# First batch's attention scores by quarters of the array, and another order of the steps ahead of the first up product

## The chip, the core and the metric

The kernel runs on one core of one Trainium2 chip. The core has TensorE (PE, with its weight loads shown as PEld), VectorE (DVE), ScalarE (ACT), GpSimd (POOL) and SyncE (SP), which here issues all loads and stores. Each engine takes its instructions in the order in which the program lists them. The metric is the device time of one execution in microseconds, lower is better.

## What is computed

Four batches of 768 tokens. Each goes through an attention of 8 heads with 64 channels, in which a token sees the tokens nearer than 16 and 24 block summaries (the maximum of 32 keys and the mean of 32 values), and then through two multiplications over tokens (rank 32) and channels (512 to 2048 and back):

```python
k_sum = k.reshape(B, H, nb, block, D).max(axis=3)
v_sum = v.reshape(B, H, nb, block, D).mean(axis=3)
scores_l = scale * np.matmul(q, k.transpose(0, 1, 3, 2))      # kept where |i - j| < 16
scores_s = scale * np.einsum('bhsd,bhnd->bhsn', q, k_sum) + np.log(block)
a = softmax(concat(scores_l, scores_s)); x = a @ concat(v, v_sum)
h = xt @ U @ V
u = x + h.transpose(0, 2, 1)
out = u + np.maximum(u @ w_ch1, 0.0) @ w_ch2
```

`U`, `V`, `w_ch1` and `w_ch2` come as 64-bit floats, and the kernel turns them into 32-bit ones itself.

## The kernel before

The work falls into stages by batch. Batch 0's attention stands ahead of everything; behind it come 16 rounds, one for each 128 hidden channels, that multiply batch 0 by the up and down weights (lines 920 and 942) while the weights are turned from 64 bits, split and stored, and while batch 1's attention goes on between the products. Batches 1 to 3 then run from the stored weights (lines 1203 and 1288).

What matters here is the part ahead of the first up product, the prologue. Its order is a list of words, `START` (line 69), that the program works through one after the other; each word makes the instructions of one step, and on each engine they stand in that order. A word is a step and its numbers:

- `lk`, `lq`, `lv`: SP loads one head's keys, one head's queries (two transfers) or two heads' values (two transfers). `lm`, `li`, `lr`, `lu`: mask, identity, a replication matrix, and U with V. `la`, `lb`: one block of 128 hidden channels of the up or of the down weights, 512 KB each, ten of them in the list.
- `K`: DVE takes the block maxima of a head's keys (line 319). `Kp` and `Kd`: POOL or DVE copies them into the gaps of the key tile (line 336).
- `S`: PE makes scores (line 354) into a bank of PSUM; a word stands for half a head, three tiles of 128 queries by 120 keys. `E`: DVE masks half a head's scores and takes the minimum (line 403), ACT takes the exponentials (line 413). `T`: PE transposes them (line 463). `C`: ACT copies them out (line 469). `V`: PE multiplies them by the values (line 480). `N`: DVE normalises a head (lines 506 to 508).
- `M` and `Mo`: PE makes the block means of two heads' values (line 293), ACT copies them out (line 307). `B` and `D` with `p`, `d` or `a`: POOL, DVE or ACT spreads them into the value tiles (line 340).
- `X`, `Xt`, `Xs`, `Xl`: U and V are scaled by ACT (line 149), turned by POOL (line 162) and DVE (lines 168, 171), and split. `Q`, `Qo`, `I`, `Io`, `J`, `Jo`, `G`, `Go`: the multiplication over tokens; `Q`, `I`, `J`, `G` are on PE (lines 1015, 666, 684, 700 and 708), the `o` steps copy out on ACT (lines 1026, 679, 692, 720) and take the rest on DVE (lines 694, 721).
- `Z`: ACT scales the weights of one round (line 149). `Y`: DVE turns them in three steps (lines 164, 168, 171). `W`: ACT rounds and DVE subtracts (lines 186, 187).
- `U0.0`: the first up product (line 920), twelve matmuls.

The queries of a head lie in a tile of 128 partitions of which every other block of 64 by 64 is zero, so that a matmul over 128 partitions gives two half tiles of 64 queries with their own keys. The function `scores` uses this: six matmuls of 128x128 weights and 120 columns for a head. A second function, `scores_by_subtiles`, leaves the zeros out: it makes 12 matmuls of 64x64 weights and 120 columns for a head, each placed on one quarter of the array, and writes two banks. Before the change only batches 2 and 3 use it (line 377 of the profile), and batch 1 uses `scores` as batch 0 does. An fp32 matmul shows as two in the profile, so a head is 12 instructions at line 354 and 24 at line 377.

The query tiles of batch 0 are four, used by heads h and h+4, so that head 7's load waits until head 3's scores are done. PSUM has 8 banks, handed out by whichever is free.

Of the kernel before, what the change touches and what calls it, by code (L numbers as in the profile page):

```python
# [16 lines left out]
B, H, S, D = 4, 8, 768, 64  # L17
DM, DF, R = 512, 2048, 32
P = 128
# [4 lines left out]
KC = NB + W  # L24
# [26 lines left out]
I32 = mybir.dt.int32  # L51
# [15 lines left out]


START = """
    lk2 lk0 K2 K0 lk1 Kp2 lq0 Kd0 li S0 lm S1 K1 lq1 Kp1 S2 lq2 S3 F lk3 E0 T0 E1 E2 S4 C0 lq3 K3 T1  # L70
    E3 E4 T2 S5 Kp3 S6 C1 S7 E5 lk4 T3 E7 lv0 K4 M0 lk5 Mo0 T4 T7 lq4 Kp4 lu C3 S8 S9 C4 lq5 T5 E6
    C2 Bp1 Dd0 X K5 Bp0 V1 T6 Dd1 E9 lv2 Kp5 Xt0 S11 E8 S10 V0 lv1 V2 E11 V3 M2 T9 E10 lk7 Mo2 lk6
    Xt1 N0 T11 lq7 C5 T8 Bp4 Xt2 lq6 M1 Dp4 lv3 C9 T10 C8 C11 C7 K7 Kp7 V9 C10 S15 Dd5 Bp5 K6 C6 Kp6
    S14 Mo1 Dp2 S12 Bp3 S13 Xs Dp3 V10 la0 la1 lb0 N1 E15 E14 V7 V6 V11 V8 T15 Bp2 la4 M3 E13 T14
    E12 Z0 T13 N5 lb1 Mo3 T12 N3 Y0.0 Xl lb2 C15 Ba7 C14 V4 Dp7 V15 V5 lr N4 Y0.1 Q0 N2 C12 Z1 Qo0
    V14 lb4 I2 N7 Io2 C13 Q1 Y0.2 Bp6 I1 Y1.0 Qo1 J2 Dp6 Jo2 la3 V12 V13 Io1 N6 Y1.1 I0 G1.2 la2 Io0
    J1 J0 I3 Jo1 Jo0 G0.2 Io3 J3 G0.1 W0 Jo3 Go0.2 Go0.1 G1.1 G0.0 G1.0 Go1.1 G0.3 Go0.0 Go0.3 Y1.2
    Go1.2 Go1.0 G1.3 Go1.3 Z2 U0.0 lb3 W1
"""


# [5 lines left out]
def body(ctx: ExitStack, tc, q0, q1, k, v, vn, uv, w1, w2, mask, ident, rep, out):  # L87
# [114 lines left out]
    def load_k(st, h):  # L202

        if st.b == 0:
            kt = kt0[h]
        else:
            kt = kv.tile([P, KTW], F32, name="kt")
        nc.sync.dma_start(out=pairs_of(kt), in_=k[st.b, :, h])
        st.kt[h] = kt

    def load_q(st, h):

        st.qt[h] = qz0[h % 4] if st.b == 0 else qz[h % 2]
        nc.sync.dma_start(out=st.qt[h][:64, 1::2], in_=q0[st.b, :, h])
        nc.sync.dma_start(out=st.qt[h][64:, 0::2], in_=q1[st.b, :, h])

    def load_qk(st, h):
        load_k(st, h)
# [5 lines left out]
    def pairs_of(kt):  # L224
        return kt[:, NB:].rearrange("p (i c) -> p i c", c=KP)[:, :, : 2 * W]
# [137 lines left out]
    def scores_by_subtiles(st, h):  # L363

        st.neg[h] = small.tile([P, NU], F32, name="neg")
        qt, kt = st.qt[h].rearrange("p u q -> p (u q)"), st.kt[h]
        ps = [bank("ps_s") for _ in range(2)]  # L370
        for i in range(3):
            for s in range(2):
                for a in range(2):
                    j = ORDER.index(2 * i + a)
                    q0, k0 = 64 + j * P + 64 * s, (j // 2) * KP + (j % 2) * KC
                    r, c = 64 * ((s + a) % 2), 64 * s
                    nc.tensor.matmul(  # L377
                        ps[a][c : c + 64, i * KC : (i + 1) * KC],
                        qt[r : r + 64, q0 : q0 + 64],
                        kt[r : r + 64, k0 : k0 + KC],  # L380
                        start=True,
                        stop=True,
                        tile_position=(r, c),
                    )
# [36 lines left out]
    def tiles_of(e):  # L421
        return e[:, : NU * KC].rearrange("p (u k) -> p u k", k=KC)
# [34 lines left out]
        nc.scalar.copy(at, ps[:KC, : 3 * P].rearrange("k (u i q) -> k u i q", i=4, q=32))  # L457

    def transposes(st, h, a):
        e = tiles_of(st.e[h])[:, 3 * a : 3 * a + 3]  # L460
        ps = bank("ps_t")
        for i in range(3):
            nc.tensor.transpose(ps[:KC, i * P : (i + 1) * P], e[:, i, :], ident_sb)  # L463
        st.ps_t[h, a] = ps

    def copies(st, h, a, copy):
# [4 lines left out]
    def values(st, h, a):  # L471
        at = st.at.pop((h, a))
        if h not in st.psx:
            st.psx[h] = bank("ps_x")
        ps = st.psx[h]
        vt = st.vt[h]
        for i in range(3):
            u = 3 * a + i
            for t in range(2):
                nc.tensor.matmul(  # L480
                    ps[64 * t : 64 * t + 64, u * DV : (u + 1) * DV],
                    at[:, i, 64 * t : 64 * t + 64],
                    vt[u % 2][:, (u // 2) * 2 + (t + u) % 2],
                    start=True,
                    stop=True,
                )
# [541 lines left out]
    def step(f):  # L1028
        return lambda i: f(st, i // 2, i % 2)

    acts = {
        "lk": lambda h: load_k(st, h),
        "lq": lambda h: load_q(st, h),
        "lm": lambda: nc.sync.dma_start(out=mask_sb, in_=mask),
        "li": lambda: nc.sync.dma_start(out=ident_sb, in_=ident),
        "lr": lambda: nc.sync.dma_start(out=rep_sb, in_=rep),
        "lv": lambda p: load_v_pair(st, p),
        "lu": lambda: nc.sync.dma_start(out=raw_uv, in_=uv.bitcast(I32)),
        "la": lambda f: load_weight(0, f),
        "lb": lambda f: load_weight(1, f),  # L1040
        "Q": spread_v,
# [399 lines left out]
```

## Time and profile before

| | |
|---|---|
| median of 3 runs | 666.86 us (666.3 to 669.9) |
| the profiled execution | 668.33 us, of which 666.5 us are its span |
| first score matmul on PE | 8.01 us |
| first up product on PE | 52.80 us |
| PE busy 10 to 35 us, 35 to 50 us | 22.15 of 25 us, 14.35 of 15 us |

Times in the profile count from the start of the span. A row of the timeline gives start, length, engine, line, operation, tiles and count, and in brackets how long the engine was idle ahead of it and what ended that. A row of the stages gives the length, then the busy time of PE, PEld, DVE, ACT and POOL with their instructions, the granted TensorE clock, the share of the 16 DMA engines in use and the GB/s that they moved. A matmul's shown length runs into the next one's, so a block's cost is taken from its start to the start of what follows.

### The profile page before, as it was taken

How to read it: one execution, taken by the hardware profiler on the slowest of the kernel's cores; microseconds unless marked ns; L12 is line 12 of the kernel's file. 1: busy time of each engine (PE TensorE's matmuls, PEld its weight loads, DVE VectorE, ACT ScalarE, POOL GpSimd, SP SyncE). 2: the span in 40 equal slices, each digit the busy share in tenths (PEclk: the TensorE clock that was granted, in tenths of full speed). 3: DMA queues.
4: the chain of work that ended last, by engine and by line, in shares of the span. 5: the costliest groups of instructions: out<-in, count | busy, mean ns of one | idle time of the engine just before them, and what ended most of it. 6: DMA issues, size and time to landing. Idle time of an engine off the chain costs nothing.

```text
span 666.5 us, 14015 instructions
## 1 busy us (share of the span) xinstructions
PE 640.6 (96%) x5232; PEld 562.6 (84%) x5232; DVE 371.7 (56%) x1006; ACT 358.5 (54%) x803; POOL 361.0 (54%) x402
## 2 busy tenths in 40 slices
PE   5899999999999898999999999999999999999997
PEld 4789889988888797997787899997787899998885
DVE  5578866668777763567544645566644521232223
ACT  4666666655553555765453467665453365553322
POOL 5424975965577676762336487662334375653310
PEclk9999999999999998999999999999999999999999
DMA  8997497766774268787457059787441055331002
GB/s 219 228 367 239 135 315 240 230 173 195 227 225 163 72 178 265 213 251 203 147 142 205 25 171 325 228 247 204 138 143 59 24 171 178 112 126 64 32 1 94
DMA packets 76420, 116.13 MB, mean 174 GB/s; under 512 B 6976, under 2 KB 52928, under 8 KB 76352
## 3 DMA queue, kind: packets, MB, share of 16 engines
q1 hardware_dynamic: 76352, 115.24, 57.1%
q8 instruction: 41, 0.67, 0.4%
q14 instruction: 27, 0.22, 0.1%
HBM read 91.10 MB, written 24.12 MB: 173 GB/s over the span
## 4 chain that ended last, share of the span: by engine, by line
PE 83%; DVE 4%; DMA 4%; ACT 3%; POOL 2%; issue 2%; SPq 1%; ACTq 0%; POOLq 0%; DVEq 0%
PE acc L1288 30%; PE ps_h L1203 25%; PE acc L942 7%; PE ps_h L920 7%; PE ps_x L494 3%; PE ps_s L354 2%; PE ps_o L739 2%; PE ps_s L377 2%; DMA place<-in_uv 1%; DMA place<-in_q 1%; PE ps_m L666 1%; DMA whole<-up 1%; PE ps_t L463 1%; PE ps_x L480 1%; POOL place L187 1%
## 5 line engine op out<-in xcount | busy, mean ns | idle before, releaser
L187 POOL TENSOR_TENSOR parts<-whole,parts 128x512 fp32r<-128x512 f32 (+1 forms) x144 | 180.5, 1262 | 160.4 <-ACT parts L186 151.3
L1288 PE MATMUL acc<-parts,gh 128*128 128x512 f32 x576 | 192.3, 399 | 0.0
L1203 PE MATMUL ps_h<-op,parts 128*128 128x384 f32 x1008 | 187.5, 340 | 3.2 <-ACT place L1262 2.9
L1203 PEld LDWEIGHTS ps_h<-op,parts 128*128 128x128 f32 x1008 | 175.4, 189 | 6.2 <-ACT place L1262 3.2
L1288 PEld LDWEIGHTS acc<-parts,gh 128*128 128x128 f32 x576 | 108.1, 188 | 23.7 <-issue 1.7
L1288 PE MATMUL acc<-parts,gl 128*128 128x512 f32 x288 | 112.6, 391 | 0.0
L1273 DVE SCALAR_TENSOR_TENSOR gl<-place,gh 128x768 fp32r<-128x768 f32 x48 | 56.2, 1171 | 97.1 <-ACT gh L1272 97.1
L186 ACT CAST parts<-whole 128x512 fp32r<-128x512 f32 (+1 forms) x144 | 83.6, 584 | 9.9 <-DMA whole<-up 8.2
L920 PE MATMUL ps_h<-place 128*128 128x384 f32 x384 | 74.5, 342 | 0.0
L1272 ACT ACTIVATE gh<-place 128x768 fp32r<-128x768 f32 x48 | 40.6, 846 | 60.0 <-PE acc L1288 59.9
L413 ACT ACTIVATE e<-e,neg 128x120 f32<-128x120 f32 x144 | 46.3, 386 | 47.4 <-DVE neg L403 45.7
L942 PE MATMUL acc<-place,gh 128*128 128x512 f32 x192 | 68.4, 410 | 1.3 <-POOL place L187 1.3
L920 PEld LDWEIGHTS ps_h<-place 128*128 128x128 f32 x384 | 65.9, 188 | 1.0 <-DVE place L721 0.3
L162 POOL TENSOR_SCALAR val<-place 128x512 f32<-128x512 f32 (+1 forms) x30 | 47.0, 1582 | 30.8 <-ACT place L149 14.2
L1288 PEld LDWEIGHTS acc<-parts,gl 128*128 128x128 f32 x288 | 54.2, 188 | 9.9 <-DVE gl L1273 0.3
L187 POOL TENSOR_TENSOR place<-val,place 128x512 fp32r<-128x512 f32 x29 | 39.4, 1378 | 18.6 <-ACT place L186 15.3
L187 POOL TENSOR_TENSOR op<-tmp,op 128x384 fp32r<-128x384 f32 x24 | 25.4, 1067 | 39.2 <-ACT op L186 39.2
L942 PEld LDWEIGHTS acc<-place,gh 128*128 128x128 f32 x192 | 35.6, 188 | 10.5 <-POOL place L187 3.2
L403 DVE CUSTOM_DVE_ANT_0 e<-ps_s,mask_sb 128x120 f32<-128x120 f32 x144 | 32.5, 276 | 13.3 <-PE ps_s L377 8.5
L942 PE MATMUL acc<-place,gl 128*128 128x512 f32 x96 | 37.6, 392 | 0.0
L932 ACT ACTIVATE gh<-ps_h 128x384 fp32r<-128x384 f32 x32 | 15.7, 490 | 36.4 <-PE ps_h L920 36.0
L1263 DVE TENSOR_TENSOR place<-place,ps_h 128x384 f32<-128x384 f32 x24 | 13.3, 553 | 38.4 <-ACT place L1262 38.3
(124 smaller groups left out, 858.8 us busy)
## 6 DMA issues: line engine op xcount, KB each, us to landing
place<-in_w SPq DMA_DIRECT2D x32, 512.0 KB, 5.6
whole<-up SPq DMA_DIRECT2D x24, 512.0 KB, 3.9
whole<-down SPq DMA_DIRECT2D x24, 512.0 KB, 3.7
whole<-up SPq DMA_DIRECT2D x24, 384.0 KB, 3.3
vt<-in_v SPq DMA_DIRECT2D x48, 146.2 KB, 4.1
kt<-in_k SPq DMA_DIRECT2D x24, 288.0 KB, 5.4
out_t<-o SPq DMA_DIRECT2D x32, 192.0 KB, 2.2
there<-squares SPq DMA_DIRECT2D x16, 384.0 KB, 4.4
```

The costliest lines, as they stand in the source:

```text
L162: nc.gpsimd.tensor_scalar(f32(bits), f32(hi), 0.0, None, ALU.mult)
L186: nc.scalar.copy(hi, val)
L187: engine.tensor_tensor(lo, val, f32(hi), ALU.subtract)
L403: nc.vector.tensor_tensor_reduce(out=e[:, u, :], in0=ps[:, i * KC : (i + 1) * KC], in1=mask_sb[:, m, :], scale=-SCALE, scalar=BIG, op0=ALU ...
L413: nc.scalar.activation(e[:, u, :], e[:, u, :], AF.Exp, bias=st.neg[h][:, u : u + 1], scale=-1.0,)
L494: nc.tensor.matmul(ps[32 * i : 32 * i + 32, u * DV : (u + 1) * DV], at[:KC, i, u], vt[u % 2][:, (u // 2) * 2 + (i // 2 + u) % 2], start=Tr ...
L920: nc.tensor.matmul(ps[:, :NH], w_split[0, f][:, c % 2, part_w, c // 2], ut[:, c, :], start=(n == 0), stop=(n == 3 * NC - 1),)
L942: nc.tensor.matmul(acc[t], gt[:, sl], w_split[1, f][:, part_w], start=(first and j == 0), stop=(last and j == 2),)
L1203: nc.tensor.matmul(ps, a[:, sa, i], b[:, sb, i], start=(first and n == 0), stop=(n == 5), skip_group_check=not first,)
L1272: nc.scalar.activation(gh, h, AF.Relu)
L1273: nc.vector.scalar_tensor_tensor(gl, h, 0.0, f32(gh), ALU.max, ALU.subtract)
L1288: nc.tensor.matmul(acc[t], gt[:, sl], w[:, part_w], start=(f == 0 and j == 0), stop=(f == NF - 1 and j == 2),)
```

## The change

The word `S` now makes a whole head with `scores_by_subtiles`, so that eight `S` words remain, all even. The transposes and the value products take their tiles in the order in which that function lays them out (`tiles_in_bank`). The list `START` is another one: other order of heads (1, 0, 3, 2, 5, 4, 7, 6), U and V loaded seventh instead of after the queries of head 4, no copy of key maxima or value summaries on DVE, and the weights loaded in another order. The loaders get an argument for the issuing engine, which stays SP. The diff without the moved numbers of lines (of `START` only its first and last lines are shown):

```diff
-    lk2 lk0 K2 K0 lk1 Kp2 lq0 Kd0 li S0 lm S1 K1 lq1 Kp1 S2 lq2 S3 F lk3 E0 T0 E1 E2 S4 C0 lq3 K3 T1
...
-    Go1.2 Go1.0 G1.3 Go1.3 Z2 U0.0 lb3 W1
+    lk1 lk0 K1 K0 lq1 Kp1 lq0 S2 lm lu li X E3 lk3 Kp0 lk2 S0 Xt0 E2 F lq3 K3 E0 Kp3 lk5 K2 Kp2 T3
...
+    Jo3 G0.2 Go0.0 G0.1 Go0.2 G0.3 Go0.1 G1.3 Go0.3 G1.1 W0 G1.2 Y1.2 Go1.1 Go1.0 lb4 Go1.2 Go1.3
+    U0.0 W1 Z2
...
     def tiles_in_bank(st, a):
-        return [3 * a + i if st.b < 2 else 2 * i + a for i in range(3)]
+        return [3 * a + i if st.b == 1 else 2 * i + a for i in range(3)]
...
     def transposes(st, h, a):
-        e = tiles_of(st.e[h])[:, 3 * a : 3 * a + 3]
+        e = tiles_of(st.e[h])
         ps = bank("ps_t")
-        for i in range(3):
-            nc.tensor.transpose(ps[:KC, i * P : (i + 1) * P], e[:, i, :], ident_sb)
+        for i, u in enumerate(tiles_in_bank(st, a)):
+            nc.tensor.transpose(ps[:KC, i * P : (i + 1) * P], e[:, u, :], ident_sb)
...
     def values(st, h, a):
-        for i in range(3):
-            u = 3 * a + i
+        for i, u in enumerate(tiles_in_bank(st, a)):
...
-        "S": step(scores),
+        "S": lambda i: scores_by_subtiles(st, i // 2),
```

On PE, from the last heads' scores (line 354 before, 377 after) to the last value products (480 before, 479 after) it stood like this; line 463 is a transpose, 293 the block means, 1015 and 1014 `Q`, 666 and 665 `I`, 684 and 683 `J`:

```order
L354 MATMUL ps_s<-place 128x120 x12
L480 MATMUL ps_x<-place 64x65 x30
L463 MATMUL ps_t<-ident_sb,gl 120x128 x3
L293 MATMUL ps_n<-place,means_w 32x65 x24
L463 MATMUL ps_t<-ident_sb,gl 120x128 x3
L463 MATMUL ps_t<-ident_sb,gh 120x128 x6
L480 MATMUL ps_x<-place 64x65 x18
L1015 MATMUL ps_v<-place,ident_sb 32x192 x8
```

and now:

```order
L377 MATMUL ps_s<-place 64x120 x12
L463 MATMUL ps_t<-ident_sb,gh 120x128 x3
L463 MATMUL ps_t<-ident_sb,gl 120x128 x3
L293 MATMUL ps_n<-place,means_w 32x65 x24
L463 MATMUL ps_t<-ident_sb,gl 120x128 x3
L463 MATMUL ps_t<-ident_sb,gh 120x128 x3
L479 MATMUL ps_x<-place 64x65 x36
L665 MATMUL ps_m<-x,u_sb 32x128 x12
L463 MATMUL ps_t<-ident_sb,gh 120x128 x3
L683 MATMUL ps_r<-t_785,rep_sb 128x128
L479 MATMUL ps_x<-place 64x65 x12
L1014 MATMUL ps_v<-place,ident_sb 32x192 x16
```

Between the last scores and the last block means stood 30 value products, and now none; behind the last block means stand 48 (36 and 12) where there were 36 (18, and 18 further on).

On DVE, around the last head's normalising (lines 506 to 508 before, 505 to 507 after) the queue stood like this; 164, 168 and 171 turn weights, 694 and 721 belong to the multiplication over tokens, 187 splits the first up weights:

```order
L171 SCALAR_TENSOR_TENSOR val<-place,val 128x512
L164 TENSOR_SCALAR val<-place 128x512 x2
L694 TENSOR_TENSOR t_st<-ps_r,t_st 64x128
L506 TENSOR_SCALAR sum<-ps_x 128x6
L507 RECIPROCAL sum<-sum 128x6
L508 TENSOR_TENSOR x<-ps_x,sum 128x6x64
L168 SCALAR_TENSOR_TENSOR val<-place,val 128x512 x2
L694 TENSOR_TENSOR t_st<-ps_r,t_st 64x128 x2
L187 TENSOR_TENSOR place<-val,place 128x2x256
L694 TENSOR_TENSOR t_st<-ps_r,t_st 64x128
L721 TENSOR_TENSOR place<-ps_u,place 128x384 x5
```

and now:

```order
L505 TENSOR_SCALAR sum<-ps_x 128x6
L506 RECIPROCAL sum<-sum 128x6
L507 TENSOR_TENSOR x<-ps_x,sum 128x6x64
L164 TENSOR_SCALAR val<-place 128x512 x2
L693 TENSOR_TENSOR t_st<-ps_r,t_st 64x128
L168 SCALAR_TENSOR_TENSOR val<-place,val 128x512 x2
L693 TENSOR_TENSOR t_st<-ps_r,t_st 64x128 x2
L171 SCALAR_TENSOR_TENSOR val<-place,val 128x512
L693 TENSOR_TENSOR t_st<-ps_r,t_st 64x128
L720 TENSOR_TENSOR place<-ps_u,place 128x384 x4
L187 TENSOR_TENSOR place<-val,place 128x2x256
```

The two sign steps, one `L171` and one `t_st` step stand behind the last normalising now instead of ahead of it.

On ACT, around the first up product's gate (`gh<-ps_h`), the scaling of the round 2 weights (line 149) stood ahead of it:

```order
L720 CAST place<-ps_u 128x384 x8
L149 ACTIVATE place<-place 128x512 x2
L932 ACTIVATE gh<-ps_h 128x384
L186 CAST place<-val 128x512
L186 CAST place<-val 128x2x256
L932 ACTIVATE gh<-ps_h 128x384
```

and now it stands behind the gate and the two roundings of the round 1 weights:

```order
L186 CAST place<-val 128x2x256
L719 CAST place<-ps_u 128x384 x4
L931 ACTIVATE gh<-ps_h 128x384
L186 CAST place<-val 128x512
L186 CAST place<-val 128x2x256
L149 ACTIVATE place<-place 128x512 x2
L931 ACTIVATE gh<-ps_h 128x384
```

On POOL the first turning step of round 2 (line 162) waits for that scaling, and the round 2 split follows from it.

More of the change, by code (lines that the diff above doesn't have):

```diff
@@ L200, in new_batch, with load_k @@
         return st
-    def load_k(st, h):
+    def load_k(st, h, by=nc.sync):
         if st.b == 0:
@@ L207, in load_k, with load_q @@
             kt = kv.tile([P, KTW], F32, name="kt")
-        nc.sync.dma_start(out=pairs_of(kt), in_=k[st.b, :, h])
+        by.dma_start(out=pairs_of(kt), in_=k[st.b, :, h])
         st.kt[h] = kt
-    def load_q(st, h):
+    def load_q(st, h, by=nc.sync):
         st.qt[h] = qz0[h % 4] if st.b == 0 else qz[h % 2]
-        nc.sync.dma_start(out=st.qt[h][:64, 1::2], in_=q0[st.b, :, h])
-        nc.sync.dma_start(out=st.qt[h][64:, 0::2], in_=q1[st.b, :, h])
+        by.dma_start(out=st.qt[h][:64, 1::2], in_=q0[st.b, :, h])
+        by.dma_start(out=st.qt[h][64:, 0::2], in_=q1[st.b, :, h])
     def load_qk(st, h):
@@ L1031, in body @@
     acts = {
[L1032 to L1035, printed above, removed]
+        **{
+            key: load
+            for e, by in (("l", nc.sync),)
+            for key, load in (
+                (e + "k", lambda h, by=by: load_k(st, h, by)),
+                (e + "q", lambda h, by=by: load_q(st, h, by)),
+                (e + "m", lambda by=by: by.dma_start(out=mask_sb, in_=mask)),
+                (e + "i", lambda by=by: by.dma_start(out=ident_sb, in_=ident)),
+                (e + "u", lambda by=by: by.dma_start(out=raw_uv, in_=uv.bitcast(I32))),
+            )
+        },
         "lr": lambda: nc.sync.dma_start(out=rep_sb, in_=rep),
         "lv": lambda p: load_v_pair(st, p),
-        "lu": lambda: nc.sync.dma_start(out=raw_uv, in_=uv.bitcast(I32)),
         "la": lambda f: load_weight(0, f),
```

13 lines of the change are left out of this document (6 added, 7 removed).

## The prediction

> **What bounds the kernel now.** The page first: PE is nearly always busy.
>
> ```profile
> span 666.5 us, 14015 instructions
> PE 640.6 (96%) x5232; PEld 562.6 (84%) x5232; DVE 371.7 (56%) x1006; ACT 358.5 (54%) x803; POOL 361.0 (54%) x402
> ```
>
> The change touches only what stands ahead of the first up product. So the stages of that part come next; columns are length, then busy time of PE, PEld, DVE, ACT, POOL, then clock, DMA share, GB/s.
>
> ```profile
> 10.00:35.00 25.00, 22.15 (x328) 20.41 (x327) 15.79 (x103) 18.67 (x59) 10.23 (x30) 1.00 1.07 229
> 35.00:50.00 15.00, 14.35 (x294) 11.82 (x294) 11.43 (x42) 9.83 (x28) 2.11 (x4) 1.00 1.03 384
> ...
> 49.90:64.90 15.00, 14.99 (x87) 13.76 (x86) 14.80 (x28) 8.64 (x21) 6.25 (x4) 1.00 0.75 222
> ```
>
> PE is busy from 10 us on, but so are the DMA engines (share 1.07 and 1.03), and from 49.9 to 64.9 us DVE (14.80 of 15). Three resources are close together here, so taking work from PE alone can't give its full price. The timeline of PE shows where the loads set the pace, and the last value load's issue, time to landing and size show when they are through:
>
> ```profile
> 8.01 4.47 PE L354 MATMUL ps_s<-place,qz 128*128 128x120 f32 x24 [8.01 <-DVE place L336]
> ...
> 24.88 1.27 PE L480 MATMUL ps_x<-place 120*64 120x65 f32 x36
> 26.08 1.58 PE L293 MATMUL ps_n<-place,means_w 96*32 96x65 f32 x48
> 27.59 0.54 PE L463 MATMUL ps_t<-ident_sb,gh 128*120 128x128 f32 x3
> ...
> 32.42 2.91 PE L354 MATMUL ps_s<-place 128*128 128x120 f32 x24 [1.14 <-DMA place<-in_q]
> 35.26 1.97 PE L480 MATMUL ps_x<-place 120*64 120x65 f32 x60
> 37.16 0.55 PE L463 MATMUL ps_t<-ident_sb,gl 128*120 128x128 f32 x3
> 37.63 1.58 PE L293 MATMUL ps_n<-place,means_w 96*32 96x65 f32 x48
> ...
> 40.27 1.55 PE L480 MATMUL ps_x<-place 120*64 120x65 f32 x36
> ...
> 46.96 0.42 PE L666 MATMUL ps_m<-x,u_sb 128*32 128x128 f32 x8 [0.60 <-issue]
> ...
> 52.80 4.63 PE L920 MATMUL ps_h<-place 128*128 128x384 f32 x24
> ...
> L236 SPq DMA_DIRECT2D place<-in_v x1: 336/336/336, 28.2 to 28.2; - x1
> ...
> DMA to landing us min/median/max: 7.9/7.9/7.9
> ...
> place<-in_v SPq DMA_DIRECT2D x8, 292.5 KB, 7.7
> ```
>
> The last value load lands at 28.2 + 7.9 = 36.1 us. PE takes up its block means (the last `M`) at 37.63, 1.5 us behind, and needs 52.80 - 37.63 = 15.17 us from there to the first up product.
>
> **The scores by quarters.** Before, a head costs half of 35.26 - 32.42 = 2.84 us, that is 1.42 us. The same function runs in batch 2:
>
> ```profile
> 233.35 0.84 PE L377 MATMUL ps_s<-kt,qz 64*64 64x120 f32 x24
> 234.13 0.55 PE L963 MATMUL ps_o<-ident_sb,r 128*128 128x128 f32 x3
> ```
>
> 24 instructions take 234.13 - 233.35 = 0.78 us from start to start, the switches of shape at both ends among them. So 0.64 us a head, 8 x 0.64 = 5.1 us of PE's work go. The Trainium skill, TensorEngine Tiling (Array Packing), Restrictions and Gotchas, speaks against this: row tiles may not work on one PSUM bank at the same time, and here the first two quarters of each tile write one bank. By that rule pairs would run in turn, a head would cost about 1.56 us (an estimate, twice the row) and nothing would be saved; the trace disagrees, since the row has just that pattern in 0.78 us.
>
> **What of this lies on the path.** PE's work ahead of the last head's scores is now 7 heads of scores (7 x 0.78 = 5.5), 11 transposes (37.16 to 37.63, 11 x 0.47 = 5.2), 3 block means (26.08 to 27.59, 3 x 1.5 = 4.5) and 8 value groups (24.88 to 26.08 is three, 8 x 0.4 = 3.2): 18.4 us. The loads are the same kilobytes as before on one queue that is never empty, and everything but the last value pair has to land ahead of that head's scores. That pair is two loads of 292.5 KB, 2.5 us at 229 GB/s, so they can't start before 36.1 - 2.5 = 33.6 us. PE starts about 0.9 us later than at 8.01, since head 1's copies now follow POOL's clears:
>
> ```profile
> 7.81 2.05 POOL L336 COPY place<-km 64x48 f32<-64x48 f32 x8
> ...
> place<-in_uv SPq DMA_DIRECT2D x1, 384.0 KB, 9.1
> ```
>
> Half of the first row behind 7.81 is 8.8 us. From 8.9 to 33.6 us PE has 24.7 us for 18.4 us of work. So these are all covered by the loads: the later start; the copies of DVE that are now POOL's (10.23 of 25 us busy); the scaling of U with V ahead of ACT's first exponentials (issued near 5 us and landing at most 9.1 us later, at 14 us, it holds ACT for at most 4 us); and the saving itself, but for the last head's 0.64 us. If that cover were not there, the whole 5.1 us would show. Of SP's order nothing else counts here: head 7's query load waits for head 3's scores, some 15 us ahead of its turn. The ten weight loads follow the values in another order; the first of them lands about 1.3 us behind the values, the last near 50 us as before, and none is due earlier than that.
>
> From the last value load on, PE does what it did from 37.63 on, with two value groups more (2 x 0.4) and without the 0.60 us of idle at 46.96, which other work fills now: 36.2 + 15.17 + 0.8 - 0.6 = 51.6 us. Value groups cost up to 0.5 us there (the row at 40.27) and 0.4 in the row at 24.88; if the less chopped order brings six of them to that, it is 51.0. The first up product starts between 51.0 and 51.6 us, 1.2 to 1.8 us earlier.
>
> **The next queue.** DVE is full from 49.9 us on, so its own end decides what PE can use. The turned weights and gates behind that:
>
> ```profile
> 44.65 0.76 DVE L164 TENSOR_SCALAR val<-place 128x512 int32<-128x512 int32 x2
> ...
> 46.49 0.56 DVE L508 TENSOR_TENSOR x<-ps_x,sum 128x384 f32<-128x384 f32 x1
> 46.97 1.28 DVE L168 SCALAR_TENSOR_TENSOR val<-place,val 128x512 int32<-128x512 int32 x2
> 48.60 0.52 DVE L694 TENSOR_TENSOR t_st<-ps_r,t_st 64x128 fp32r<-64x128 f32 x2 [0.35 <-ACT t_st L692]
> 49.91 0.69 DVE L187 TENSOR_TENSOR place<-val,place 128x512 fp32r<-128x512 f32 x1 [0.80 <-ACT place L186]
> ...
> 53.48 1.28 DVE L171 SCALAR_TENSOR_TENSOR val<-place,val 128x512 int32<-128x512 int32 x2
> 54.68 1.48 DVE L721 TENSOR_TENSOR place<-ps_u,place 128x384 fp32r<-128x384 f32 x3
> ...
> 58.88 1.12 DVE L168 SCALAR_TENSOR_TENSOR val<-place,val 128x512 int32<-128x512 int32 x1
> ```
>
> Before, DVE went from the last normalising (46.49 + 0.56 = 47.05) to the last `L721` (54.68 + 1.48 = 56.16) in 9.1 us, with 1.15 us of waits. Now `L164` (0.76), one `L171` (0.64) and one `t_st` (0.26) stand behind the normalising too, so the work there is 0.76 + 4 x 0.26 + 1.28 + 3 x 0.64 + 0.69 + 8 x 0.49 = 9.6 us, and I allow 0.5 us of waits. On PE the last value product follows the start of the block means at 36.2 us after 1.5 us for these, three transposes (1.4), eight value groups (3.2) and two `I` and a `J` (some 0.4 each): 43.5 us. The normalising behind it (0.9 us in the trace) ends near 44.5. That makes 54.6 us against 56.16: 1.5 us earlier.
>
> **The scaling moved behind the gate.** What the first POOL step of round 2 waits for, and where POOL's split holds PE up:
>
> ```profile
> 53.98 1.27 ACT L149 ACTIVATE place<-place 128x512 f32<-128x512 f32 x2
> 55.14 0.48 ACT L932 ACTIVATE gh<-ps_h 128x384 fp32r<-128x384 f32 x1
> 55.51 1.14 ACT L186 CAST place<-val 128x512 fp32r<-128x512 f32 x2
> ...
> 54.84 3.05 POOL L162 TENSOR_SCALAR val<-place 128x512 f32<-128x512 f32 x2 [13.33 <-DMA qz<-in_q]
> ...
> 66.05 2.52 POOL L187 TENSOR_TENSOR place<-val,place 128x512 fp32r<-128x512 f32 x2 [4.24 <-ACT place L186]
> ...
> 67.39 0.73 PE L942 MATMUL acc<-place,gh 128*128 128x512 f32 x2 [0.46 <-POOL place L187]
> ```
>
> The gate stood 55.14 - 52.80 = 2.34 us behind the first up product. With that product at 51.3 it is at 53.6, the roundings end at 55.1, the scaling gives its first half at 55.7 and POOL's first step ends at 57.2, its second at 58.7. DVE's next step, at 58.88 before, is due at 57.4: POOL is just in time, the slack of 2.5 us that it had (56.4 against 58.88) is used up. So POOL's split at 66.05 moves with DVE, by 1.5 us. PE is held there already (0.46 us), so a gain of PE beyond DVE's is lost at 67.39. **Sum: 1.5 us.** Behind that stage PE is the bound, and it carries the gain to the end. The profiled execution took 668.33 us with its span of 666.5, so its sum is 666.8; it lies 1.5 us above the median of the three runs (666.3 to 669.9). From the median I forecast **665.4 us**, 664.6 to 666.2 by the bounds of the terms (0.7 to 2.3 us).
>
> **The rivals.** 0.5%, about what a measurement of this kernel can tell from no change, is 3.3 us.
>
> *Loads faster.* From 10 to 35 us they move 229 GB/s and from 35 to 50 us 384; I found no engine that makes them slow. If the new mix (U with V early, values spread differently) lifts that rate by a tenth, the last value lands 2.5 us earlier, and with DVE's tail behind it the gain is 4 us: 662.9. It decides from a landing before 34.3 us. For it: the rate does vary with what is in flight. Against it: the same packets, and the queue full all the time.
>
> *Absorbed.* ACT's scaling behind the gate makes POOL late by 1 to 1.5 us instead of just in time, or the block means' copy holds up ACT's queue ahead of the last exponentials. Then PE waits longer at 67.39 and the end is where it was: 666.8. It decides when POOL's split stays at 66 us.
>
> *Slower: the clock.* PE now waits for loads, and where it did so before its clock fell:
>
> ```profile
> 14.70:18.10 3.40, 2.19 (x24) 1.81 (x23) 2.42 (x19) 2.81 (x9) 0.25 (x2) 1.00 1.11 242
> ...
> 253.60:257.00 3.40, 1.08 (x6) 1.09 (x7) 0.92 (x2) 3.36 (x9) 2.69 (x4) 1.00 1.08 308
> 257.00:260.50 3.50, 3.50 (x13) 3.50 (x12) 1.07 (x2) 1.54 (x4) 3.29 (x7) 0.51 0.79 246
> ```
>
> A stretch of 3.4 us with 1.08 us of PE work was followed by one at 0.51 of the clock; one with 2.19 was not. PE's share ahead of 33.6 us falls to 18.4 of 24.7, 2.5 us in 3.4, so single stretches will lie between those two. Each at half clock costs up to 1.7 us, covered while the loads are late, and on the path from about 31 us on. With two of them there the gain of 1.5 us turns into a loss of 1.9: 668.8. It decides where a stretch ahead of the last block means has less than some 1.6 us of work. The Trainium skill, TensorE: Matmul & The Clock Gate, Part 1, has the gate close after an idle window of about 3.4 us; the idle time here was shorter (3.40 less 1.08 us in its stretch), so the rows see it close sooner than that. By that rule this case would hardly arise, for none of the waits worked out above is so long.
>
> **How the numbers follow.** The forecast has a chance of 0.53 (with PE's or DVE's term off by a microsecond among it), loads faster 0.15, absorbed 0.18, the clock 0.14. The range of 8 in 10 reaches from inside the faster case to inside the clock's: 662.6 to 667.8. Faster by over 0.5% (below 663.5) is most of the second case: 0.15. Slower by over 0.5% (above 670.2) needs three stretches at half clock: 0.05. The rest, 0.80, is no change that can be told.
>
> **What would show it.** Right: eight score blocks of about 0.8 us; the last value landing at 36 us; PE idle ahead of 36 us for some 6 us with `DMA` behind it; the first up product at 51.0 to 51.6; the last `L720` ending near 54.6; POOL's split at 64.5. Wrong: a landing more than 1.5 us from 36; a clock below 1.00 between 14 and 40 us; POOL's split at 66 with PE waiting over 2 us there; or any difference of more than a microsecond that arises behind 80 us.

## The result, and the profile after

| | before | after |
|---|---|---|
| median of 14 runs each, beside one another | 667.47 us (664.86 to 669.92) | 671.62 us (669.15 to 674.95) |
| ratio, 95% interval | | 1.0065 (1.0046 to 1.0084) |
| profiled execution, its span | 668.33 us, 666.5 us | 672.31 us, 670.5 us |
| first score, first up product | 8.01, 52.80 us | 8.19, 58.33 us |

The changed kernel is slower by 0.65%, above the forecast range. PE's busy time hardly moved, though it has 96 matmuls more; the line of the page after the change:

```profile
PE 640.9 (96%) x5328; PEld 559.8 (83%) x5328; DVE 366.8 (55%) x999; ACT 359.0 (54%) x803; POOL 364.1 (54%) x409
```

The loss shows in PE's timeline ahead of the first up product:

```profile
27.60 0.85 PE L377 MATMUL ps_s<-place,qz 64*64 64x120 f32 x24
28.37 1.62 PE L479 MATMUL ps_x<-place 120*64 120x65 f32 x48
29.92 0.54 PE L463 MATMUL ps_t<-ident_sb,gl 128*120 128x128 f32 x3
30.39 0.56 PE L479 MATMUL ps_x<-place 120*64 120x65 f32 x10
34.33 1.70 PE L479 MATMUL ps_x<-place 120*64 120x65 f32 x26 [3.37 <-issue]
35.95 1.48 PE L377 MATMUL ps_s<-place 64*64 64x120 f32 x24
37.36 0.89 PE L463 MATMUL ps_t<-ident_sb,gl 128*120 128x128 f32 x3
...
38.83 2.07 PE L293 MATMUL ps_n<-place,means_w 96*32 96x65 f32 x48
40.82 0.85 PE L377 MATMUL ps_s<-place 64*64 64x120 f32 x24
41.60 0.54 PE L463 MATMUL ps_t<-ident_sb,gh 128*120 128x128 f32 x3
...
42.40 1.58 PE L293 MATMUL ps_n<-place,means_w 96*32 96x65 f32 x48
43.91 0.54 PE L463 MATMUL ps_t<-ident_sb,gl 128*120 128x128 f32 x3
...
44.71 2.02 PE L479 MATMUL ps_x<-place 120*64 120x65 f32 x61
48.02 0.57 PE L479 MATMUL ps_x<-place 120*64 120x65 f32 x11 [1.28 <-issue]
...
58.33 2.94 PE L919 MATMUL ps_h<-place 128*128 128x384 f32 x16
...
73.92 0.73 PE L941 MATMUL acc<-place,gh 128*128 128x512 f32 x2 [0.60 <-POOL place L187]
```

A head's scores take 28.37 - 27.60 = 0.77 us, as forecast. But in the middle of a value group, ten matmuls into it, PE stops for 3.37 us, and once more for 1.28 us. Nothing that the profile shows is waited for ("issue"): the ten matmuls before and the 26 behind it belong to the same tiles. The stages of the same stretch, with the granted clock as the third column from the end:

```profile
12.60:16.00 3.40, 1.98 (x29) 1.13 (x28) 3.03 (x23) 2.29 (x8) 2.01 (x8) 1.00 1.12 236
16.00:22.80 6.80, 5.36 (x74) 4.67 (x78) 1.61 (x11) 3.76 (x13) 1.88 (x6) 0.50 1.11 213
29.70:33.10 3.40, 1.26 (x23) 0.88 (x20) 1.55 (x8) 2.66 (x10) 1.77 (x9) 1.00 1.08 216
33.10:39.90 6.80, 5.57 (x76) 4.81 (x77) 2.13 (x15) 1.61 (x5) 0.00 (x0) 0.50 1.02 338
```

Two stretches of 3.4 us with little work for PE, 1.98 and 1.26 us, are each followed by 6.8 us at half clock. In the second of these the scores at 35.95 take 1.41 us to the next row instead of 0.77. What stands between 31 and 33.2 us on the DMA queues, when PE waits:

```profile
q1 hardware_dynamic: 209, 0.47, 102.0%
q8 instruction: 1, 0.02, 4.3%
```

One packet of kind "instruction", 16384 bytes, served from 31.46 to 32.98 us; PE goes on 1.35 us behind its end. There are 42 such packets (41 before), one for about every 256 of PE's instructions. That gave the theory to be tested, called A: PE had used up the instructions that it had been given, and the next block of them (its refill) had not come.

### The profile page after: what moved, and what is told of

It is laid out like the page before. It is cut to its first block, busy times and chain, and to the rows that moved or that the text cites. A ratio compares the mean times of both kernels' runs of the same rounds, so it can differ in the third digit from the quotient of the medians.

```text
span 670.5 us, 14220 instructions
## 1 busy us (share of the span) xinstructions
PE 640.9 (96%) x5328; PEld 559.8 (83%) x5328; DVE 366.8 (55%) x999; ACT 359.0 (54%) x803; POOL 364.1 (54%) x409
## 4 chain that ended last, share of the span: by engine, by line
PE 80%; issue 4%; DMA 4%; ACT 4%; DVE 3%; POOL 2%; SPq 1%; ACTq 0%; POOLq 0%; DVEq 0%
PE acc L1293 30%; PE ps_h L1208 23%; PE acc L941 8%; PE ps_h L919 6%; PE ps_x L493 3%; PE ps_s L377 2%; DMA whole<-up 2%; PE ps_o L738 2%; PE ps_t L463 2%; DMA place<-in_v 1%; PE ps_s L354 1%; PE ps_n L293 1%; POOL val L162 1%; POOL place L187 1%; PE ps_m L665 1%
## 5 line engine op out<-in xcount | busy, mean ns | idle before, releaser
L941 PE MATMUL acc<-place,gh 128*128 128x512 f32 x192 | 68.4, 410 | 1.6 <-POOL place L187 1.5
L931 ACT ACTIVATE gh<-ps_h 128x384 fp32r<-128x384 f32 x32 | 15.7, 490 | 36.4 <-PE ps_h L919 36.0
```

Source lines behind the costliest of these rows:

```text
L941: nc.tensor.matmul(acc[t], gt[:, sl], w_split[1, f][:, part_w], start=(first and j == 0), stop=(last and j == 2),)
```

## The experiments

A is set against C (the new order is slow in itself), D (the quarters are slow in this place), and later F (the loads alone decide). Each run has a 95% interval against the kernel before on the same chip; times of different runs are compared by these ratios.

**The new order with the scores by the whole array (e1).**

```diff
-        "S": lambda i: scores_by_subtiles(st, i // 2),
+        "S": lambda i: (scores(st, i // 2, 0), scores(st, i // 2, 1)),
-        return [3 * a + i if st.b == 1 else 2 * i + a for i in range(3)]
+        return [3 * a + i if st.b < 2 else 2 * i + a for i in range(3)]
```

> The new order with the scores by the whole array, as before the change: 12 matmuls a head in place of 24 in batch 0, so 192 fewer instructions on PE (96 matmuls, 96 weight loads) ahead of the first up product. Theory A (PE runs out of instructions: it has used 256 since the last block of them and the next block has not come): with fewer instructions the waits that the trace calls issue shrink from 3.4 and 1.3 us to under 1 us each, the first up product comes at 52 to 55 us, and the time is 666 to 669 us. Theory C (the new order itself, whatever the scores): the first up product stays at 57 to 59 us and the time at 671 to 673 us.

667.8 us, ratio 0.9994 (0.9974 to 1.0015). No wait with issue behind it over 0.25 us is left, the clock is full from 13.5 to 255 us, and the first up product comes at 51.38 us. So the order by itself costs nothing: C falls. PE's rows from the first up product on:

```profile
51.38 4.65 PE L919 MATMUL ps_h<-place 128*128 128x384 f32 x24
...
66.90 0.73 PE L941 MATMUL acc<-place,gh 128*128 128x512 f32 x2 [0.60 <-POOL place L187]
```

Of 52.80 - 51.38 = 1.4 us that the order gains, only 67.39 - 66.90 = 0.5 us reach the matmul behind POOL's split.

**The order of before with the scores by quarters (e2).** Of a head's two words `S` the first one in `START` stays, and makes the whole head by `scores_by_subtiles`; the rest is as after the change.

> The order of before with the scores by quarters: of a head's two words only the one that stood first is kept. Theory A: the 192 instructions more bring a wait of over 1.5 us with issue behind it at instruction 705 or 961 of PE, and the time is 668 to 672 us. Theory C: no such wait, the time is that of the kernel before or up to 1.5 us less. Theory D (the quarters are slow in this place): a head takes over 1.1 us at the full clock.

669.66 us, ratio 1.0031 (1.0006 to 1.0057). PE's timeline:

```profile
27.60 0.71 PE L293 MATMUL ps_n<-place,means_w 96*32 96x65 f32 x17
31.06 1.62 PE L293 MATMUL ps_n<-place,means_w 96*32 96x65 f32 x31 [2.75 <-issue]
...
35.94 1.30 PE L479 MATMUL ps_x<-place 120*64 120x65 f32 x30
38.89 1.09 PE L479 MATMUL ps_x<-place 120*64 120x65 f32 x30 [1.65 <-issue]
...
45.31 0.22 PE L479 MATMUL ps_x<-place 120*64 120x65 f32 x1 [1.02 <-issue]
```

Three waits, in other steps than after the change: in the block means, and ahead of a group's last matmul. The stages between them count PE's instructions, matmuls first, weight loads second:

```profile
0.00:31.05 31.05, 19.43 (x338) 15.01 (x339) 18.95 (x107) 16.84 (x50) 16.17 (x47) 1.00 0.96 225
31.05:38.87 7.82, 6.18 (x124) 5.17 (x124) 3.06 (x25) 4.75 (x16) 2.96 (x9) 0.78 1.03 304
38.87:45.29 6.42, 5.40 (x125) 4.76 (x125) 4.02 (x12) 4.25 (x10) 1.86 (x3) 1.00 1.03 405
```

677 instructions to the first wait, then 248 and 250. With PE's semaphore instructions, which the rows leave out, 705, 961 and 1217 instructions have started ahead of the one that waits: 256 apart. (Instruction 705 below is the one with 705 ahead of it.) After the change it is 705 and 1217 as well:

```profile
0.00:34.30 34.30, 19.81 (x337) 15.83 (x338) 14.87 (x98) 17.47 (x51) 19.32 (x58) 0.88 0.99 224
34.30:48.00 13.70, 12.40 (x249) 10.81 (x248) 7.19 (x40) 7.21 (x21) 3.54 (x7) 0.80 1.02 372
```

D falls too: the heads took 0.8 us where the clock was full.

**The count moved, the program not (e3).** Small matmuls on zeros stand ahead of the first score (32 of them; 64 in the second run):

```diff
+    ps = bank("ps_d")
+    for _ in range(32):
+        nc.tensor.matmul(ps[:64, :8], qz0[0][:64, 0, :64], qz0[0][:64, 0, :8], start=True, stop=True)
     first = []
     for word in START.split():
```

> After the change, with 32 small matmuls on zeros (64 weights by 64, 8 columns, 128 instructions with their weight loads) that PE does ahead of the first score, whose result nobody reads. Theory A: the waits with issue behind them stay at instructions 705 and 1217 of PE as counted from the start, so in the program they come half a block sooner; the ten value products that ended at 31 us run through. Theory C or a wait for data that the trace does not name: the wait stays at the same place of the program (ahead of the same value products), at count 833. Time 668 to 674 us by either.

> The same with 64 small matmuls (256 instructions, one whole block). Theory A: the waits stand at counts 705, 961 or 1217, which are the old places of the program again but of other blocks; the wait of 3.4 us at count 705 is gone or short, since that count is now reached at some 22 us, and one at 961 may take its place. Otherwise the wait stays where it is in the program, as it would by theory A for 961. So this run alone tells little; beside the one with 32 it shows whether the place follows the count. Time 669 to 674 us.

With 32: 670.66 us, ratio 1.0052 (1.0031 to 1.0074). The value group that broke at 31 us runs through, and the waits stand in the block means and in a later value group:

```profile
30.34 1.27 PE L479 MATMUL ps_x<-place 120*64 120x65 f32 x36
...
33.82 1.46 PE L293 MATMUL ps_n<-place,means_w 96*32 96x65 f32 x43 [0.35 <-issue]
...
40.16 0.43 PE L463 MATMUL ps_t<-ident_sb,gh 128*120 128x128 f32 x2 [1.20 <-ACT place L469]
...
46.39 0.33 PE L479 MATMUL ps_x<-place 120*64 120x65 f32 x3 [0.94 <-issue]
```

These are instructions 961, 1217 and 1473. The middle one is put down to ACT, but it too is the first of a block. With 64, one block: 677.11 us, ratio 1.0121 (1.0068 to 1.0173), waits of 3.31 us ahead of the same value products as after the change, where the count is now 961, and of 1.74 us at 1729. With 32 I had expected the waits at 705 and 1217, and 705 passed without one; but the wait did not stay at its place in the program either (count 833), as it would have for missing data. The run with 64 says little by itself, since a whole block brings the wait back to its old place, and it is slower than the 674 us that I had allowed.

The traces taken together say more. Over all 17 kernels profiled here, each of the 17 waits over 0.25 us ahead of 80 us that has issue behind it stands at 705, 961, 1217, 1473 or 1729. Setting the packets beside these marks in order (the first with 449, the second with 705, and so on) shows the other half: at the 102 marks from 449 to 1729, no block begins sooner than 1.22 us behind the end of its packet, and the 17 waits end 1.22 to 1.64 us behind it. So these waits are for the packets.

**Fewer instructions in another step (e6).** One matmul makes the block means of two heads:

```diff
-            for h in (2 * p, 2 * p + 1):
-                r = 32 * (h % 4)
-                nc.tensor.matmul(
-                    ps[r : r + 32, :DV],
...
+            nc.tensor.matmul(
+                ps[:32, : 2 * DV],
+                means_w[:rows, i, n : n + 32],
+                vt0[p][i][:rows, :, (u // 2) * 2 + t],
...
-        nc.scalar.copy(st.vsum[p // 2][r : r + 64], st.ps_n.pop(p)[r : r + 64, :DV])
+        ps = st.ps_n.pop(p)
+        for i in range(2):
+            nc.scalar.copy(st.vsum[p // 2][r + 32 * i : r + 32 * i + 32], ps[:32, i * DV : (i + 1) * DV])
```

> After the change, with the block means of two heads made by one matmul of 130 columns in place of two of 65 (12 matmuls a pair of heads in place of 24; ACT copies them out in two pieces): 192 instructions fewer on PE ahead of the first up product, as many as the quarters added, with the quarters kept. Theory A: the waits with issue behind them come to under 1.5 us in all, the clock stays full from 31 us on, the first up product comes at 51 to 54 us, the time is 665 to 668.5 us. If the quarters or the order are slow in themselves: the first up product stays behind 56 us and the time at 670 to 673 us.

671.8 us, ratio 1.0079 (1.0045 to 1.0114), with the first up product at 58.95 us: a miss, and both numbers are those that I had given for quarters or an order slow in themselves. But the edit isn't neutral, and a wait stayed:

```profile
21.61 2.88 PE L291 MATMUL ps_n<-place,means_w 96*32 96x130 f32 x24
24.42 0.85 PE L377 MATMUL ps_s<-place,qz 64*64 64x120 f32 x24
...
34.49 0.67 PE L377 MATMUL ps_s<-place 64*64 64x120 f32 x4 [2.70 <-issue]
```

24 matmuls of 130 columns take 2.81 us from start to start, where 48 of 65 take 1.51 (42.40 to 43.91 after the change): the two heads, on two column groups, had run beside each other. So the run adds some 5 us of work (four such pairs), and does not separate what it was made for. The wait is at 705 again, though the program has come further by then: the count sets where PE may stop, not how long.

**Fewer loads in flight (e5, e9, e8).** After the change SP has up to eight transfers in flight, as read from issues and landings in the trace. Here SP waits ahead of a load of keys, values or weights until the third such load before has landed:

```diff
+        n = len(landed) - 3
+        if n >= 0:
+            nc.sync.dma_start(out=probes[n : n + 1], in_=landed[n])
         acts[name](*map(int, filter(None, word[len(name) :].split("."))))
```

`landed` holds 16 bytes of each loaded tile, so the small transfer can't be issued before that tile is there.

> After the change, with SP held back ahead of each load of keys, values or weights in the list until the third such load before it has landed (a transfer of 16 bytes out of that load's tile stands ahead of it; nothing else is altered), so that fewer loads stand in the DMA engines' queues. Theory A with the refill standing behind the loads: the refill begins within 3 us of its block being due, where it took 4 to 6 us; the waits with issue behind them come to under 1 us in all, the first up product to 52 to 54 us, if the loads keep their rate (last value landing by 37.5 us); time 665 to 668 us. If the refill's delay has nothing to do with the loads: waits of 3 and 1 us stay at counts 705 and 1217, time 670 to 673 us. If the loads lose their rate, the last value lands later than 38 us and the waits have DMA behind them.

663.61 us, ratio 0.9945 (0.9918 to 0.9972): faster than both kernels, and 1.4 us better than A said. PE from 24.62 us on, and the same value group:

```profile
24.62:50.06 25.44, 25.44 (x537) 22.34 (x534) 20.42 (x96) 21.21 (x62) 9.19 (x25) 1.00 0.90 263
```

```profile
29.82 1.27 PE L479 MATMUL ps_x<-place 120*64 120x65 f32 x36
...
50.06 4.75 PE L919 MATMUL ps_h<-place 128*128 128x384 f32 x24
```

PE never stops. The packet that came at 31.46 us, 6.3 us behind instruction 449, now comes at 25.40, 0.8 us behind it. From the value group to the first up product PE needs 50.06 - 29.82 = 20.2 us, after the change 58.33 - 30.39 = 27.9. PE's instructions, their order and their number are the same: with the refill ahead of its need the two waits and the half clock behind the first are gone, and the hold on the loads brought it forward.

Two other depths were run with this edit, two and six.

> As e5, held back until the second such load before has landed. Theory A: the refill begins within 2.5 us, no wait with issue behind it. The loads may lose rate: 662 to 664 us if the last value lands no later than in e5, up to 668 us if it lands 2 to 4 us later, with DMA behind PE's waits.

> As e5, held back until the sixth such load before has landed: the same small transfers, but hardly a hold, since some seven loads stand in the queue anyway. Theory A: the refill is late again, waits with issue behind them of 2 us or more in all, time 668 to 673 us. If the small transfers themselves or their waits make the difference: 662 to 665 us as e5.

At two: 666.3 us, ratio 0.9978 (0.9957 to 0.9999), no wait with issue behind it, but one of 0.99 us for the replication matrix, which now stands behind held weights. At six: 665.68 us, ratio 0.9975 (0.9956 to 0.9995), no wait either, the first up product at 51.23 us. That is a miss: I took six for no hold. The small transfers stand in the queue like the others, and never more than eight were in flight without them, so this run may hold back more than six suggests and is no control; that they help in another way than by thinning the loads is not excluded.

**The kernel before and the quarters alone, held (e7, e10, e11, e13).** The same edit on the kernel before, and on the order of before with the quarters:

> The kernel before with SP held back as in e5 (until the third load before has landed). Theory A (the quarters are worth what was forecast, and only the refill took it away): the wait of 0.6 us at instruction 1217 goes, the first up product comes at 51.5 to 52.5 us, the time is 665 to 668 us, so that the change is worth 1 to 3 us where the refill is prompt (e5 against this run). Theory F (holding the loads back is itself what made e5 fast, by a better use of the DMA engines): this run gains 3 to 5 us over the kernel before, 663 to 664 us, and the change is worth nothing there.

> The order of before with the scores by quarters (e2), held back as in e5. Theory A: the three waits with issue behind them (5.4 us in e2) shrink to under 1 us, the first up product comes at 50 to 52.5 us where e2 had 56.3, the time is 663.5 to 667 us.

669.22 us, ratio 1.0028 (1.0007 to 1.005), and 668.65 us, ratio 1.0005 (0.9985 to 1.0025). Both are slower than any theory had it, and both run into a new wait, here the second one's:

```profile
45.04 0.46 PE L683 MATMUL ps_r<-t,rep_sb 128*128 128x128 f32 x2 [3.18 <-DMA rep_sb<-in_rep]
```

In the order of before the 64 KB of the replication matrix stand behind six weight loads of 512 KB. In e10 the waits for instructions (5.4 us in e2) are gone as A said, and this one eats the gain. In e7 one of 1.42 us at 961 stays, with held weight loads in flight, beside one of 2.49 us for the matrix. Moving `lr` ahead of `la0` mends the order:

> e7 (the kernel before, held back until the third load before has landed) with the replication matrix loaded ahead of the weights, so that PE's wait of 2.5 us for it goes. Theory A (the change is worth what was forecast where the refill is prompt): the first up product comes at 52 to 54 us, the time is 665.5 to 668 us, 2 to 4 us over e5. Theory F (the holding back made e5 fast): 662.5 to 664.5 us, as e5.

> The order of before with the scores by quarters, loads held back as in e5 and the replication matrix ahead of the weights: e11 with quarters and nothing else. Theory A, with the gain of the quarters lost to the new order's waits at the start in e5: PE has 5 us less work than in e11 and must wait for loads instead, the first up product comes at 48 to 50 us, the time is 661 to 663.5 us, up to 2.5 us under e11. Theory F (all that counts is the loads): no less than e11, 663 to 665 us.

The kernel before: 663.68 us, ratio 0.9936 (0.9909 to 0.9962), the first up product at 49.81 us. With the quarters alone: 662.94 us, ratio 0.9923 (0.9902 to 0.9943), 49.73 us, with 1.35 us of a wait at 705 left. F's number came out for the first: held loads give the kernel before as much as the changed one, and the 1 to 3 us that A gave the change where the refill is prompt can't be told here (0.9945 against 0.9936). The second is where A put it and the fastest of all, but 0.7 us under the first is within their intervals. Nor does the prologue show a gain (49.73 against 49.81 us). Half of e11's ten runs have a granted clock of 0.997, like the profiled one, which has 3.4 us at half clock at 252 us (see "Behind 80 us" below). The runs with 0.998 or more have a median of 662.8 us in e5 (three of five) and e13 (three of four) and of 662.9 in e11 (five of ten). So where the loads are held, the quarters are worth nothing that can be told.

And the hold does not act on the refill alone. The kernel before had lost 0.60 us to it, and gains 3.0 us at the first up product: its wait of 1.14 us for queries (32.42 us) is gone too, and 1.5 us more of PE's work is done by 24.62 us (16.37 against 14.90). The stages say why the quarters gain nothing, the changed kernel held (e5) first, then the kernel before held (e11):

```profile
0.00:24.62 24.62, 14.23 (x212) 11.43 (x215) 9.85 (x66) 10.71 (x31) 13.66 (x40) 0.86 0.93 233
```

```profile
0.00:24.62 24.62, 16.37 (x170) 15.54 (x172) 15.02 (x91) 13.74 (x40) 13.72 (x40) 1.00 0.94 234
24.62:49.80 25.18, 25.18 (x484) 22.28 (x481) 20.10 (x76) 18.27 (x53) 7.12 (x18) 1.00 0.86 260
```

From 24.62 us on both have PE full for some 25 us. Up to there, the changed one spends what the quarters save: 2.1 us more without work, and part of the rest at half clock.

**The count alone, raised (e12, e14, e15).** Two attempts to give the kernel before 192 more instructions and nothing else: three tiny matmuls behind each half head, and each score matmul cut into two of 60 columns (this one also held, with the early `lr`).

```diff
+        for _ in range(3 if st.b == 0 else 0):
+            nc.tensor.matmul(ps[:64, 480:484], qt[:64, 64:128], kt[:64, NB : NB + 4], ...)
```

```diff
+            n = KC // 2 if st.b == 0 else KC
+            for c in range(0, KC, n):
                 nc.tensor.matmul(
-                    ps[:, i * KC : (i + 1) * KC],
+                    ps[:, i * KC + c : i * KC + c + n],
...
```

> The kernel before, order and scores untouched, with three very small matmuls (64 weights by 64, 4 columns, into columns of the bank that nobody reads) behind each half head's scores in batch 0: 192 more instructions on PE, as many as the quarters add, and some 3 us of PE's work, most of it in the waits for loads. Theory A: waits with issue behind them of 2 us or more in all at counts 705, 961 or 1217, the first up product at 55 us or later, time 669 to 672 us. Theory C or D (order or quarters are slow in themselves, the count is not): no such wait beyond the 0.6 us, 667 to 669 us.

> The kernel before, order and array use untouched, with each score matmul of batch 0 cut into two of 60 columns: 192 instructions more on PE, as many as the quarters add, at about the same work, without the tiny matmuls that held the clock low in e12. Theory A: waits with issue behind them of 2 us or more in all at counts 705, 961 or 1217, the first up product at 54.5 us or later, 668.5 to 672 us. Theory C or D: no wait beyond the 0.6 us of before, 667 to 668.5 us.

> e14 with the loads held back and the replication matrix early, that is e11 with the scores cut in halves. Theory A: the waits with issue behind them are under 0.5 us in all, the first up product at 49.5 to 52 us, 663.5 to 665.5 us: the 192 instructions cost little where the refill is prompt. Otherwise the same loss over e11 as e14 shows over the kernel before.

681.0 us (1.018, 1.0123 to 1.0236), 683.86 us (1.0233, 1.0212 to 1.0254) and 681.6 us (1.0201, 1.0179 to 1.0224): all far off. PE got much slower by itself, with first up products at 68.4, 70.4 and 68.5 us (see the last section), so that a late refill still came in time; the waits at 1217 are 0.90 and 0.75 us in the first two, none in the third. They don't test the count. The test of it is left to e1, the shifted kernels and the marks.

## Why the prediction was wrong

**The loads and the blocks: right.** The last value load landed 7.9 us behind its issue at 28.5 us, at 36.4 (36.1 forecast), and a head took 0.77 us at full clock. PE's waits for loads ahead of 36 us, put at some 6 us, came to 2.3 (1.68 at 16.85 us, 0.59 at 18.09). The rule of the Trainium skill on row tiles in one bank (TensorEngine Tiling (Array Packing), Restrictions and Gotchas) again did not show.

**"So these are all covered by the loads": the step that failed.** It took PE to be limited by data, engines and its own work. The supply of PE's instructions is a fourth limit, and the change loads it: 24 matmuls in 0.77 us where there were 12 in 1.42. It cost two waits of 3.37 and 1.28 us, and the half clock behind the first. The place for it was in the prediction: the row at 46.96 us with 0.60 us of idle and issue behind it. I read it as a gap that "other work fills now". It was instruction 1217. From the last block means on, "PE does what it did" held in its size (42.40 to 58.33 is 15.9 us, without the second wait 14.65; 15.4 were forecast), but those means began at 42.40 us and not at 36.2.

**The sum.** The first up product came 58.33 - 51.3 = 7.0 us behind the forecast. The two waits are 3.37 + 1.28 = 4.65 us. The half clock between 34.33 and 40.82 us cost 2.6 us: 26 value products 0.78 (1.62 us, where 48 took 1.55 from 28.37 on), the scores 0.64 (1.41 for 0.77), six transposes 0.67 (1.47 for the 0.80 from 41.60 on), the block means 0.48 (1.99 for the 1.51 from 42.40 on). Together 7.2 us.

**The next queue: DVE right, POOL not.** These are DVE's rows after the change:

```profile
51.74 0.56 DVE L507 TENSOR_TENSOR x<-ps_x,sum 128x384 f32<-128x384 f32 x1
...
59.94 1.94 DVE L720 TENSOR_TENSOR place<-ps_u,place 128x384 fp32r<-128x384 f32 x4
```

From 52.30 to 61.88 us it is 9.6 us, the sum of the work, without the 0.5 us of waits that I had allowed; it ends 7.3 us behind the forecast because the normalising came late with PE. POOL's split was said to be just in time behind ACT's moved scaling:

```profile
72.59 2.53 POOL L187 TENSOR_TENSOR place<-val,place 128x512 fp32r<-128x512 f32 x2 [2.98 <-ACT place L186]
```

It begins 72.59 - 58.33 = 14.3 us behind the first up product, where it was 66.05 - 52.80 = 13.25. In e1 it is 65.56 - 51.38 = 14.2, and e13, which has ACT's old order, has 62.78 - 49.73 = 13.05. So the *absorbed* rival was real, at 1.0 us, and the forecast gain of the order is mostly lost there even without the waits.

**Behind 80 us** a part came back, which I had called a sign against me. PE's row in batch 2, before and after:

```profile
255.92 6.02 PE L1203 MATMUL ps_h<-op,parts 128*128 128x384 f32 x24 [2.87 <-ACT place L1262]
```

```profile
261.33 4.46 PE L1208 MATMUL ps_h<-op,parts 128*128 128x384 f32 x24 [1.53 <-ACT place L1267]
```

A wait of 1.53 us in place of 2.87 left the clock full, so of 6.5 us at the split (73.92 against 67.39) 4.0 are left at the end. The kernel before does either by itself: of its 89 runs beside the experiments, 47 have a granted clock of 0.997, as the profiled one has with its 3.4 us at half clock, and a median of 668.2 us; 24 have 0.999 or more, and 665.6 us. So this part comes and goes without the change, by more than the forecast gain. Whether the change makes the shorter wait more frequent wasn't tried.

**The clock rival** had the right sign and trigger: it named a stretch with less than 1.6 us of work ahead of the last block means, and there is one with 1.26 (the other, with 1.98, lies above that mark and was followed by half clock too). It had the wrong cause, waits for loads, and too small a price, since the wait that closes the clock is itself lost on the path. Its chance of 0.14, and 0.05 for slower by over 0.5%, came from pricing the clock without that wait.

## What to carry to other kernels

A wait with "issue" behind it in the middle of a group of alike matmuls is worth a count of the instructions ahead of it, and a look at the packets of kind "instruction". Here such waits stood at steps of 256 and ended with a packet: the engine was out of instructions, and halving a block's time by twice as many instructions made it worse. It came mostly where many short instructions met seven or eight loads in flight, and it could be met from the side of the loads: issuing a load only when the third before it had landed took 1.2% off the changed kernel, and 0.6% off the kernel before once the replication matrix was loaded earlier. After such a hold, look for a small transfer that now stands behind large ones.

## What the runs showed of the hardware

**Instructions come in blocks, and late where many loads are in flight.** The packets are of 16384 bytes, and the waits 256 instructions apart. Take as a packet's mark the instruction that opens the block ahead of its own (193 for the packet of 449, 449 for that of 705). How long behind its mark a packet starts varies. Up to the mark 1473 of the kernels before and after, e1 and e2 it was 0.5 to 0.6 us where two to five loads were in flight (behind 65.73 us before, 54.06 after), and 2.0 to 6.3 us with seven or eight, with one exception of 0.7. The number of loads does not settle it: behind the mark 1729 after the change (77.02 us) it was 2.1 us with two to four in flight, and under the hold still 4.3 us in e13 (mark 449) and 4.4 us in e7 (mark 705). PE went on some 1.35 us behind the packet's end. The Trainium skill, Runtime: NRT & Kernel Launch, Instruction fetch mechanics, has blocks of 256 instructions fetched while the one before runs, and says that crossing a boundary is mostly hidden. The period of 256 agrees; the 3.37 us here are not hidden.

**A busy PE is not always given its clock.** With the score matmuls cut in halves (e14), PE's rows show no idle time from 7.28 us to beyond 40, yet the same three transposes are slow for over 20 us (0.85 us at 17.84, 0.49 at 33.90):

```profile
7.28 10.77 PE L356 MATMUL ps_s<-place,qz 128*128 128x60 f32 x48 [7.28 <-DMA qz<-in_q]
17.84 0.85 PE L465 MATMUL ps_t<-ident_sb,gh 128*120 128x128 f32 x3
...
33.90 0.49 PE L465 MATMUL ps_t<-ident_sb,gl 128*120 128x128 f32 x3
34.22 2.79 PE L356 MATMUL ps_s<-place,qz 128*128 128x60 f32 x24
```

No granted clock is on record there ahead of 33.8 us, where it is full; before the change the first record is a full one at 11.3 us. In e12 it comes at 32.7 us, and I had put that down to the tiny matmuls, which e14 does not have. The Trainium skill, TensorE: Matmul & The Clock Gate, Part 1, gives the slow start about 3.4 us of time, whatever is issued. This trace shows over 20. What decides stays open. After it, 24 matmuls of 60 columns still take 2.6 us (34.22 to 36.84), 0.11 us each, and in e1 twelve of 120 columns 1.4 us (20.11 to 21.54), 0.12 us each: with weights of 128 by 128, half the columns saved next to nothing.
